# Two throw-away tiles for the squares, and a hand-built order with new constants

## The chip, the core and the metric

The kernel runs on one core of a Trainium2 chip. The core has five engines that run side by side, each through its own list of instructions in order: TensorE (PE, matrix products), VectorE (DVE), ScalarE (ACT, pointwise functions, copies and sums along a row), GpSimd (POOL) and SyncE (SP, which issues DMA transfers). They wait for each other by semaphores. TensorE's array can be used in parts; here two halves work on different things at once. The metric is the device time of one execution in microseconds (us), the median of several.

## What is computed

Four batches of 12608 tokens with 128 channels pass through an attention over 32 induced points in both directions, and every token then goes through a layer with 1024 hidden values:

```
def mab(q, kv):                                  # attention, softmax over the keys
    a = softmax(scale * q @ kv.T);  return a @ kv
h = mab(inducing, x)                             # 32 points look at all tokens of a batch
y = mab(x, h)                                    # each token looks at the 32 points
h1 = y @ w_in                                    # 128 -> 1024
solu = h1 * softmax(h1)
ln = (solu - mean(solu)) / sqrt(var(solu) + 1e-6) * g_ln
out = ln @ w_out                                 # 1024 -> 128
```

## The kernel before

Tokens are worked on in tiles of 128, 99 to a batch, 396 in all. Each tile goes round a ring of engines: PE forms the first layer (L974) into one of two PSUM buffers; DVE scales it, writes it to a row buffer and takes the row's extreme (L1009); ACT takes the exponential into a buffer `eu`, with its row sum (L1019); POOL multiplies the two (L1023); ACT squares the product for the variance and keeps only the row sum, so the squares themselves go to a throw-away tile `sq` (L1034); DVE transposes the product (L1047). Four tiles make a group; PE multiplies a transposed group by the output weights (L1093) in two streams, one on each half. The streams' results gather in two PSUM banks over three groups and are then evacuated to a tile of raw results by DVE or ACT (L1118), the variance is finished on ACT and POOL (L1145 to L1165), and the scaled output is written by ACT in four activations or by POOL in one operation (L1180, L1176) and stored. The function `p1` does the first attention of the next batch meanwhile, `p2` the second attention, twelve tiles at a time.

Nothing is scheduled on the chip. A `Planner`, when the program is built, keeps a clock for every engine, takes each step's cost from a number in the code, and writes out the instructions in the order in which its model would start them. Among steps that are ready within `SLACK` of the earliest it takes the one with the lowest priority number; the constants `PR_...` are offsets in tiles to that number, `P1_...`, `P2_...`, `LATE`, `WIN`, `WOUT` and `RUSH` place the work of the attentions and the weights, and `FILL` says from which gap on PE is kept busy with throw-away transposes. Where a step has an alternative (`alt`), the planner takes the engine that suits. `AFTER` is the delay from the end of a step on one engine to a start on another. The engines then run these lists in order. `HN_MORE` says how many of the spare buffers, left when the raw results have theirs, become row buffers.

Three lines carry the step that the change touches most:

```
sq = buf([P, FF], "sq", BF16)
...
"ACT", 1040, lambda: nc.scalar.activation(sq, e, AF.Square, scale=1.0 / 32.0, accum_out=G["qe"][:, s, 0:1]), d,
```

Of the kernel before, what the change touches and what calls it, by code (L numbers as in the profile page):

```python
# [10 lines left out]
BF16 = mybir.dt.bfloat16  # L11
U32 = mybir.dt.uint32
I32 = mybir.dt.int32
AF = mybir.ActivationFunctionType
# [5 lines left out]
P = 128  # L20
C = 128
M = 32
FF = 1024
# [5 lines left out]
JB = FF // M  # L29
BEAT = 224  # L30
SWITCH = 310


def cut(total, most, unit):
# [13 lines left out]
DIRECT = 3  # L48
EUS = 5
SPARES = 8  # L50
H_LAST = -34.17
TURNS = 3
ODD = 1
HN_MORE = 5
RAWS = 2
FILL = 358.31
FIRST = 4
LATE = -7.63
P1_FROM = 9.25
P1_GO = -11.78  # L60
P1_STEP = 6.49
P2_AHEAD = 40.84
P2_START = 24
PR_EX = 1.43
PR_EV = -19.77
PR_FI = 11.4
PR_G2 = -2.26
PR_HN = -3.18
PR_MU = -2.16
PR_SQ = 14.63  # L70
PR_SA = 24.36
PR_SP = 15.35
PR_ED = 14.54
PR_EA = -9.6
PR_TU = 2.38
RUSH = 2.52
TURN_NS = 62
PARTS = {"PE": ("PE0", "PE1")}
SLACK = {"PE": 17, "ACT": 71, "DVE": 138, "POOL": 33, "SP": 0}
SPARE = 150  # L80
WARM = 32
WOUT = -6.79
WIN = -19.36

AFTER = {
    "PE": {"PE": 0, "ACT": 237, "DVE": 236, "POOL": 240, "SP": 290},
# [16 lines left out]
class Done:  # L103


    def __init__(self, eng, end):
        self.eng, self.end = eng, end


class Op:  # L110
    def __init__(self, eng, cost, fn, *after, prio=None, alt=None, moves=0):
        self.eng, self.cost, self.fn, self.after, self.prio, self.alt, self.moves = eng, cost, fn, after, prio, alt, moves


class Event:
# [19 lines left out]
class Planner:  # L135
# [97 lines left out]
    def run(self):  # L233
        clock = self.clock
        while self.ops:
            first = min(self.ops, key=lambda o: (max(self.free(o[0].eng), o[1]), o[3]))
            eng = first[0].eng
            limit = max(self.free(eng), first[1]) + self.slack[kind(eng)]
            same = {eng, "PE"} if eng in PARTS["PE"] else {eng, *PARTS.get(eng, ())}
            pick = min(  # L240
                (o for o in self.ops if o[0].eng in same and o[1] <= limit),
                key=lambda o: (o[2][1] if o[0].prio is None else o[0].prio, o[3]),
            )
            self.ops = [o for o in self.ops if o[3] != pick[3]]
            op, ready, task = pick[:3]
            eng = op.eng
            start = max(self.free(eng), ready)
            if kind(eng) == "PE" and start - self.free("PE") > FILL:
                self._fill(start - SPARE)
            self.now = start  # L250
            op.fn()
            end = start + (self._pe(start, op.cost) if kind(eng) == "PE" else op.cost)
            for e in PARTS.get(eng, (eng,)):
                clock[e] = end
            if eng == "SP":
                end = self.data = max(end + DMA_LAG, self.data) + op.moves / DMA_RATE
            done = Done(eng, end)
            self._step(task, done)
        assert not self.blocked, "the plan is stuck"
# [3 lines left out]
def set_attention_then_solu_kernel(ctx: ExitStack, tc: tile.TileContext, x, inducing, w_in, w_out, g_ln, out):  # L263
    nc = tc.nc
    NB, N, _ = x.shape
    scale = 1.0 / float(C) ** 0.5
# [29 lines left out]
    def buf(shape, name, dtype=F32, where=None):  # L296
        return (where or const).tile(shape, dtype, name=name)

    def bufs(n, shape, name, dtype=F32):
        return [buf(shape, f"{name}{i}", dtype) for i in range(n)]  # L300
# [17 lines left out]
    where = bank_pool.__enter__()  # L318
    bank_e = [buf([P, 512], f"bank_e{i}", where=where) for i in range(8)]
    hn_b = bufs(3, [P, FF], "hn")  # L320
    sq = buf([P, FF], "sq", BF16)

    eu_b = buf([P, EUS, FF], "eu")
    xT_b = buf([C, PG, P], "xT")
# [143 lines left out]
    def weights_out():  # L468
# [11 lines left out]
        for k in range(KC):  # L480
            d = yield Op("ACT", 251, gain(k), g, gd, prio=LATE)
        g = [d]
        mp, rel = yield H

        def mean():
            for k in range(KC):
                nc.tensor.matmul(mp[:, :C], lhsT=ones_mean, rhs=wg[:, k, :], start=(k == 0), stop=(k == KC - 1))

        d = yield Op("PE", KC * 215, mean, g, rel, prio=LATE)
        d = yield Op(  # L490
# [3 lines left out]
            ),  # L494
            d, prio=LATE,
        )
# [7 lines left out]
        for a in range(4):  # L504
            for q in range(4):
                c = yield dma(
                    M * FF * 4,
                    lambda: nc.sync.dma_start(rows[a * M : (a + 1) * M, :, q, :C], wg[q * M : (q + 1) * M]), d, o, issue=600, prio=LATE,
                )
# [69 lines left out]
    def p1(b, k):  # L579
# [87 lines left out]

        d = yield Op("PE", (0 if early else SWITCH) + n * (72 if early else 60), scores, ready, rel, ind_ready.after)

# [18 lines left out]
        )  # L688
        d = yield Op("PE", (280 if early else SWITCH) + 110, lambda: nc.tensor.matmul(mq, lhsT=fold2, rhs=v["mdiag"], start=True, stop=True), d)
        first = k == 0  # L690
# [157 lines left out]
    def p2(b, j):  # L848
# [26 lines left out]

        d = yield Op("PE", 72 * n if direct else SWITCH + n * 60, scores, d, rel, hd)
        if not direct:
# [72 lines left out]
    def PRIO_P1(b, k):  # L950
        return -20.0 + k if b == 0 else NT * (b - 1) + P1_FROM + P1_STEP * k + P1_GO

# [3 lines left out]
    def main():  # L956
        for t, (b, j, s) in enumerate(tiles):
            for item in starts.get(t, ()):
                spawn(*item)
            G = grp[(b, j)]  # L960
            if s == 0:
                spawn(open_group(b, j), t)
            ka, i = part_of[b, ff_groups[j][0] + s]
            aT_d = yield aT_ready[(b, ff_groups[j][0] + s)]
            hw_d = yield hw_ready[b]
            hp, rel = yield H.at(t + H_LAST)
            A = aT_of[(b, ka)]
            aT, hs = A["aT"][0], hT[b][1]

            def halves():  # L970
                for k in range(2):
                    rows = slice((i % 2 * 2 + k) * M, (i % 2 * 2 + k + 1) * M)
                    cols = slice(k * 512, (k + 1) * 512)
                    nc.tensor.matmul(hp[:, cols], lhsT=aT[rows, i // 2, :], rhs=hs[rows, cols], start=True, stop=True)  # L974

            d = yield Op(f"PE{i % 2}", 870, halves, aT_d, hw_d, rel, prio=t - 50)
            if t + 1 == len(tiles) or tiles[t + 1][0] != b:
                give(HW, hT[b], d)
            spawn(soft(t, hp, d), t)
# [19 lines left out]
    def soft(t, hp, d):  # L999
        b, j, s = tiles[t]  # L1000
        G = grp[(b, j)]
        ka, i = part_of[b, ff_groups[j][0] + s]
        A = aT_of[(b, ka)]
        hn, rel = yield HN
        nm, mrel = yield NM
        rn = A["aT"][1][:, i : i + 1]
        d = yield Op(
            "DVE", 1208,
            lambda: nc.vector.tensor_scalar(out=hn, in0=hp, scalar1=rn, scalar2=None, op0=ALU.mult, op1=ALU.min, accum_out=nm),  # L1009
            d, rel, mrel, prio=t + PR_HN,  # L1010
        )
        give(H, hp, d)
        A["left"] -= 1
        if not A["left"]:
            give(AT, A["aT"], d)
        srel = yield G["st"]
        e, rel = yield EU
        de = yield Op(
            "ACT", 1133, lambda: nc.scalar.activation(e, hn, AF.Exp, bias=nm, scale=-1.0, accum_out=G["qe"][:, s, 1:2]), d, rel, srel,  # L1019
            prio=t + PR_EX,  # L1020
        )
        give(NM, nm, de)
        d = yield Op("POOL", 2330, lambda: nc.gpsimd.tensor_tensor(out=e, in0=hn, in1=e, op=ALU.mult), de, prio=t + PR_MU)  # L1023
        give(HN, hn, d)
        left = []

        def over(d):
            left.append(d)
            if len(left) == 2:
                give(EU, e, *left)  # L1030

        def square():
            ds = yield Op(
                "ACT", 1040, lambda: nc.scalar.activation(sq, e, AF.Square, scale=1.0 / 32.0, accum_out=G["qe"][:, s, 0:1]), d,  # L1034
                prio=t + PR_SQ,
            )
            G["squared"].append(ds)
            over(ds)
            if len(G["squared"]) == ff_groups[j][1]:
                yield from floor(b, j)  # L1040

        spawn(square(), t)
        n = ff_groups[j][1]
        rel = yield G["vt"]
        dt = yield Op(
            "DVE", 1163,
            lambda: nc.vector.transpose(  # L1047
                out=G["vtb"][:, : n * FF].rearrange("p (j s t) -> p j s t", j=M, s=n)[:, :, s, :],
                in_=e.rearrange("p (a f) -> p a f", f=M),
            ),  # L1050
            d, rel, prio=t + PR_TU,
        )
        over(dt)
        G["turned"].append(dt)
        if len(G["turned"]) == n:
            for w in range(2):
                spawn(products(b, j, t, w), t)
# [158 lines left out]
    for b in range(NB):  # L1216
        if b:
            for k in range(NP):
                starts.setdefault(NT * (b - 1) + int(P1_FROM + P1_STEP * k), []).append((p1(b, k), PRIO_P1(b, k)))
        starts.setdefault(max(0, NT * (b - 1)), []).append((combine(b), PRIO_P1(b, NP - 1) if b else -28))  # L1220
# [3 lines left out]
    def handover():  # L1224
# [23 lines left out]
        for i in range(at, SPARES):  # L1248
            give(HN if i < at + HN_MORE else EU, spare[:, more + i * FF : more + (i + 1) * FF], *done)
        for v in vt_b:  # L1250
# [51 lines left out]
```

## Time and profile before

| | us |
|---|---|
| median of 3 runs (lowest, highest) | 1207.19 (1206.87, 1208.22) |
| the profiled execution | 1207.56 |
| its span, first to last instruction | 1205.7 |
| PE busy, matmul | 1162.4 (96%) |
| ACT busy | 1138.5 (94%) |
| DVE busy | 1104.9 (92%) |
| POOL busy | 1073.9 (89%) |

A line of busy time is the time in which at least one instruction of that engine ran. PE counts as busy when either half works. An activation that accumulates shows as two rows, the activation itself and the read of its accumulator; neighbouring rows may overlap. In the timeline a row has start, duration, engine, line, operation, output and inputs, shape and count, and in brackets the idle time ahead of it with what ended it.

### The profile page before, as it was taken

How to read it: one execution, taken by the hardware profiler on the slowest of the kernel's cores; microseconds unless marked ns; L12 is line 12 of the kernel's file. 1: busy time of each engine (PE TensorE's matmuls, PEld its weight loads, DVE VectorE, ACT ScalarE, POOL GpSimd, SP SyncE). 2: the span in 40 equal slices, each digit the busy share in tenths (PEclk: the TensorE clock that was granted, in tenths of full speed). 3: DMA queues.
4: the chain of work that ended last, by engine and by line, in shares of the span. 5: the costliest groups of instructions: out<-in, count | busy, mean ns of one | idle time of the engine just before them, and what ended most of it. 6: DMA issues, size and time to landing. Idle time of an engine off the chain costs nothing.

```text
span 1205.7 us, 69282 instructions
## 1 busy us (share of the span) xinstructions
PE 1162.4 (96%) x30901; PEld 1041.7 (86%) x30901; DVE 1104.9 (92%) x1727; ACT 1138.5 (94%) x2396; POOL 1073.9 (89%) x790
## 2 busy tenths in 40 slices
PE   9889999999999999999999999999999999999996
PEld 7558989898899898888898988988888988889896
DVE  6799999999999999999999999999999999999992
ACT  5588999999999999999999999999999999999994
POOL 2678998889999999989799999999889999999994
PEclk9879999999999999999999999999999999999999
DMA  9453334432223433242223334233211212221011
GB/s 352 176 134 89 87 91 127 127 92 72 74 74 86 133 116 93 80 130 88 73 75 91 94 94 136 78 117 116 83 47 50 80 39 57 56 57 38 21 31 44
DMA packets 134252, 111.49 MB, mean 92 GB/s; under 512 B 79009, under 2 KB 87105, under 8 KB 133825
## 3 DMA queue, kind: packets, MB, share of 16 engines
q1 hardware_dynamic: 133952, 107.06, 30.4%
q8 instruction: 242, 3.96, 1.4%
q14 instruction: 58, 0.47, 0.1%
HBM read 53.51 MB, written 51.39 MB: 87 GB/s over the span
## 4 chain that ended last, share of the span: by engine, by line
PE 22%; ACT 19%; DVE 9%; issue 6%; POOL 1%; DMA 1%; SPq 0%; ACTq 0%; POOLq 0%; DVEq 0%
PE op L1093 17%; ACT eu L1019 8%; ACT sq L1034 7%; DVE vt L1047 3%; PE h L974 2%; DVE hn L1009 2%; DVE spare L1009 2%; ACT os L1180 1%; POOL eu L1023 1%; PE h L546 1%; ACT spare L1118 1%; DVE spare L1118 1%; ACT aT L915 1%; DMA dd<-qe 0%; ACT xT L608 0%
## 5 line engine op out<-in xcount | busy, mean ns | idle before, releaser
L1093 PEld LDWEIGHTS op<-wc,vt 32*128 32x128 f32 x25600 | 939.7, 186 | 63.0 <-issue 32.6
L1093 PE MATMUL op<-wc,vt 32*128 32x129 f32 x25600 | 978.6, 274 | 15.8 <-ACT spare L1118 6.6
L1023 POOL TENSOR_TENSOR eu<-spare,eu 128x1024 f32<-128x1024 f32 x249 | 586.2, 2373 | 27.3 <-ACT eu L1019 27.3
L1047 DVE STREAM_TRANSPOSE vt<-eu 128x1024 f32<-128x1024 f32 x396 | 484.8, 1233 | 7.1 <-POOL eu L1023 6.9
L1034 ACT ACTIVATE sq<-eu 128x1024 bf16<-128x1024 f32 x396 | 415.7, 1050 | 16.0 <-POOL eu L1023 4.4
L974 PE MATMUL h<-hs,aT 32*128 32x512 f32 x1584 | 416.2, 617 | 8.4 <-DVE spare L1009 3.0
L1023 POOL TENSOR_TENSOR eu<-hn,eu 128x1024 f32<-128x1024 f32 x147 | 346.4, 2371 | 16.4 <-ACT eu L1019 15.8
L1009 DVE TENSOR_SCALAR_CACHE_REDUCE spare<-h,rn 128x1024 f32<-128x1024 f32 x249 | 311.6, 1257 | 18.8 <-PE h L974 11.2
L1019 ACT ACTIVATE eu<-spare,nm 128x1024 f32<-128x1024 f32 x249 | 283.4, 1139 | 5.8 <-DVE spare L1009 4.8
L1009 DVE TENSOR_SCALAR_CACHE_REDUCE hn<-h,rn 128x1024 f32<-128x1024 f32 x147 | 184.2, 1259 | 12.8 <-PE h L974 10.6
L1019 ACT ACTIVATE eu<-hn,nm 128x1024 f32<-128x1024 f32 x147 | 167.3, 1139 | 0.7 <-DVE hn L1009 0.6
L974 PEld LDWEIGHTS h<-hs,aT 32*128 32x128 f32 x1584 | 124.6, 189 | 33.7 <-issue 8.6
L1180 ACT ACTIVATE os<-spare,fin 128x128 f32<-128x128 f32 (+1 forms) x264 | 82.9, 389 | 1.2 <-POOL fin L1165 1.2
L1034 ACT ACTIVATION_READ_ACCUMULATOR sq<-eu 128x1 f32 x396 | 74.6, 188 | 0.0
L1019 ACT ACTIVATION_READ_ACCUMULATOR eu<-spare,nm 128x1 f32 x249 | 47.0, 189 | 0.0
L546 PE MATMUL h<-ident,xn 32*128 32x32 f32 x1188 | 46.1, 219 | 0.8 <-issue 0.6
L546 PEld LDWEIGHTS h<-ident,xn 32*128 32x128 f32 x1188 | 45.2, 137 | 0.8 <-ACT xT L608 0.3
L1118 DVE COPY spare<-op 128x774 f32<-128x774 f32 (+1 forms) x31 | 27.5, 888 | 19.2 <-PE op L1093 12.0
L546 PEld LDWEIGHTS h<-ident,a 32*128 32x128 f32 (+1 forms) x800 | 34.5, 138 | 10.3 <-issue 3.2
L887 POOL TENSOR_TENSOR s<-s,mx 128x384 f32<-128x384 f32 (+3 forms) x37 | 28.7, 775 | 14.4 <-DVE mx L884 14.3
L608 ACT COPY xT<-h 128x768 f32<-128x768 f32 (+2 forms) x54 | 39.4, 729 | 1.1 <-PE h L546 1.0
L546 PE MATMUL h<-ident,a 32*128 32x32 f32 (+1 forms) x800 | 37.1, 219 | 3.2 <-DVE hn L1009 1.7
(160 smaller groups left out, 762.1 us busy)
## 6 DMA issues: line engine op xcount, KB each, us to landing
out_dram<-os SPq DMA_DIRECT2D x96, 256.0 KB, 2.5
xT<-xd SPq DMA_DIRECT2D x93, 256.0 KB, 3.2
xn<-in_x_dram SPq DMA_DIRECT2D x73, 256.0 KB, 3.0
xd<-xT SPq DMA_DIRECT2D x73, 256.0 KB, 2.6
dl<-dd SPq DMA_DIRECT2D x396, 1.0 KB, 2.7
xd<-vt SPq DMA_DIRECT2D x6, 768.0 KB, 10.4
spare<-in_x_dram SPq DMA_DIRECT2D x5, 768.0 KB, 10.7
wc<-hn SPq DMA_DIRECT2D x16, 128.0 KB, 3.0
```

Of the source, the lines that this page charges most:

```text
L546: nc.tensor.transpose(out=tr[:h, at : at + M], in_=block[rows, :h], identity=ident[rows, rows])
L608: nc.scalar.copy(in_rows(xT[:, :n, :], c0), from_rows(tr, n))
L887: lambda: nc.gpsimd.tensor_tensor(out=s2[:, :n, :], in0=s2[:, :n, :], in1=mx[:, :n].unsqueeze(2).to_broadcast([P, n, M]), op=ALU.subtract),
L974: nc.tensor.matmul(hp[:, cols], lhsT=aT[rows, i // 2, :], rhs=hs[rows, cols], start=True, stop=True)
L1009: lambda: nc.vector.tensor_scalar(out=hn, in0=hp, scalar1=rn, scalar2=None, op0=ALU.mult, op1=ALU.min, accum_out=nm),
L1019: "ACT", 1133, lambda: nc.scalar.activation(e, hn, AF.Exp, bias=nm, scale=-1.0, accum_out=G["qe"][:, s, 1:2]), d, rel, srel,
L1023: d = yield Op("POOL", 2330, lambda: nc.gpsimd.tensor_tensor(out=e, in0=hn, in1=e, op=ALU.mult), de, prio=t + PR_MU)
L1034: "ACT", 1040, lambda: nc.scalar.activation(sq, e, AF.Square, scale=1.0 / 32.0, accum_out=G["qe"][:, s, 0:1]), d,
L1047: lambda: nc.vector.transpose(out=G["vtb"][:, : n * FF].rearrange("p (j s t) -> p j s t", j=M, s=n)[:, :, s, :], in_=e.rearrange("p (a f) ...
L1093: nc.tensor.matmul(op[:rows, a - 2 * w, i * (C + 1) : (i + 1) * (C + 1)], lhsT=vt[q, k, :], rhs=wc[q, k, :], start=(k == 0), stop=(k == JB ...
L1118: return lambda: eng(F["raw"][:rows, : 4 * k, :].rearrange("p (j a) c -> p j a c", a=4)[:, :, 2 * w : 2 * w + 2].rearrange("p j a c -> p a ...
L1180: nc.scalar.activation(os[:rows, q, :], raw[:, q, :], AF.Copy, scale=y[:, i0 + q : i0 + q + 1])
```

## The change

The squares write two tiles in turn instead of one; a step can have a `tail`, a time by which the planner takes its result as ready later, and the first layer gets one of 80 ns; and most of the planner's constants have new values.

```
-H_LAST = -34.17
+H_LAST = -36.3
-HN_MORE = 5
+HN_MORE = 7
-FILL = 358.31
+FILL = 419.69
-LATE = -7.63
-P1_FROM = 9.25
-P1_GO = -11.78
+LATE = -20.28
+P1_FROM = 8.96
+P1_GO = -8.64
-PR_G2 = -2.26
...
-PR_SQ = 14.63
-PR_SA = 24.36
-PR_SP = 15.35
...
+PR_G2 = 4.93
...
+PR_SQ = 12.45
+PR_SA = 21.51
+PR_SP = 7.52
...
-RUSH = 2.52
+RUSH = 9.95
...
-SLACK = {"PE": 17, "ACT": 71, "DVE": 138, "POOL": 33, "SP": 0}
+SLACK = {"PE": 60, "ACT": 59, "DVE": 137, "POOL": 0, "SP": 0}
...
+            end += op.tail
             done = Done(eng, end)
...
-    sq = buf([P, FF], "sq", BF16)
+    sq_b = bufs(2, [P, FF], "sq", BF16)
...
-            d = yield Op(f"PE{i % 2}", 870, halves, aT_d, hw_d, rel, prio=t - 50)
+            d = yield Op(f"PE{i % 2}", 870, halves, aT_d, hw_d, rel, prio=t - 50, tail=TAIL)
...
+            def into():
+                sq_b.reverse()
+                nc.scalar.activation(sq_b[0], e, AF.Square, scale=1.0 / 32.0, accum_out=G["qe"][:, s, 0:1])
+
+            ds = yield Op("ACT", 1040, into, d, prio=t + PR_SQ)
```

The numbers of lines grow by 2 or 3 in the new file (L1034 is L1037, L1118 is L1121). The order of the instructions changes on every engine. Two places show how.

ACT near the end of the program, before: `sq` is the throw-away tile, `eu` a buffer of products, `fin` the small tiles of the variance, `x2` two equal rows on end.

```order
L1034 ACTIVATE sq,qe_104<-eu 128x1024
L1034 ACTIVATE sq,qe_106<-eu 128x1024
L1019 ACTIVATE eu,qe_108<-spare,nm_115 128x1024
L1019 ACTIVATE eu,qe_108<-spare,nm_116 128x1024
L1180 ACTIVATE os_101<-spare,fin_113 128x128 x4
L1034 ACTIVATE sq,qe_106<-eu 128x1024 x2
L1019 ACTIVATE eu,qe_108<-spare,nm_117 128x1024
L1034 ACTIVATE sq,qe_106<-eu 128x1024
L1034 ACTIVATE sq,qe_108<-eu 128x1024 x3
```

Five of these squares stand directly behind another one and write what it wrote. ACT in the same stretch now, with `sq_83` and `sq_84` the two tiles:

```order
L1037 ACTIVATE sq_84,qe_105<-eu 128x1024
L1037 ACTIVATE sq_83,qe_107<-eu 128x1024
L1021 ACTIVATE eu,qe_109<-spare,nm_116 128x1024
L1183 ACTIVATE os_102<-spare,fin_114 128x128 x4
L1021 ACTIVATE eu,qe_109<-spare,nm_117 128x1024
L1037 ACTIVATE sq_84,qe_107<-eu 128x1024
L1037 ACTIVATE sq_83,qe_107<-eu 128x1024
L1021 ACTIVATE eu,qe_109<-spare,nm_118 128x1024
L1037 ACTIVATE sq_84,qe_107<-eu 128x1024
L1037 ACTIVATE sq_83,qe_109<-eu 128x1024
L1037 ACTIVATE sq_84,qe_109<-eu 128x1024
L1037 ACTIVATE sq_83,qe_109<-eu 128x1024
```

Neighbouring squares no longer write the same tile. In the whole program a square stands directly behind a square 146 times before and 117 times now; of these, 146 and 30 wait on ACT's own semaphore.

ACT at the first evacuation, in the first batch, before (`op` is a bank of products, `spare` here the raw results):

```order
L1034 ACTIVATE sq,qe_102<-eu 128x1024
L1118 COPY spare<-op_667 128x2x3x129
L1118 COPY spare<-op_668 128x2x3x129
L1145 ACTIVATE fin_111<-dl_110,tiny 128x12
L1146 ACTIVATE fin_111<-spare 128x12
```

Both banks are evacuated by ACT, one behind the other. ACT at the same place now:

```order
L1037 ACTIVATE sq_83,qe_103<-eu 128x1024
L1121 COPY spare<-op_673 128x2x3x129
L1148 ACTIVATE fin_112<-dl_111,tiny 128x12
L1021 ACTIVATE eu,qe_105<-hn_82,nm_115 128x1024
L1149 ACTIVATE fin_112<-spare 128x12
```

ACT has one of the two. DVE has the other, between a transpose of `p1` (`ew`) and one of the ring (`vt`), and stands so:

```order
L1050 STREAM_TRANSPOSE vt<-eu 128x32x32
L1011 TENSOR_SCALAR hn_82,nm_115<-h_671,rn_96 128x1024
L737 STREAM_TRANSPOSE ew<-eT 128x384
L1121 COPY spare<-op_672 128x2x3x129
L1050 STREAM_TRANSPOSE vt<-eu 128x32x32
```

The second evacuation has moved to DVE. Over the program ACT has 41 evacuations before and 33 now, DVE 31 and 39; ACT 264 and 256 output scalings, POOL 34 and 36; DVE 21 and 24 of the running sums of `p1`, POOL 15 and 12. All other counts are the same, but for a few throw-away transposes on PE.

## Rows read from the trace of the kernel before

**Rows 1.** Busy time of each engine by stage; (x) is the number of instructions.

```profile
core 0: us, PE busy (x) PEld busy (x) DVE busy (x) ACT busy (x) POOL busy (x), PEclk, DMA share, GB/s
50.60:343.20 292.60, 286.39 (x7357) 248.19 (x7358) 271.67 (x429) 278.14 (x574) 261.88 (x179) 0.95 0.35 98
343.20:628.60 285.40, 281.93 (x7778) 255.02 (x7776) 273.02 (x426) 280.55 (x589) 263.79 (x195) 1.00 0.34 96
628.60:914.80 286.20, 281.88 (x7778) 256.16 (x7774) 272.53 (x426) 281.12 (x593) 264.82 (x194) 0.99 0.33 95
914.80:1180.00 265.20, 251.95 (x7012) 235.06 (x7008) 248.82 (x330) 260.35 (x548) 254.92 (x181) 0.98 0.17 45
1180.00:1206.00 26.00, 15.24 (x509) 14.66 (x501) 4.13 (x5) 10.12 (x28) 8.59 (x18) 0.91 0.14 40
```

**Rows 2.** Waits of ACT, 343.2 to 628.6 us: us in total, times, longest us.

```profile
ACT eu L1019 <- DVE spare L1009: 0.6, 1, 0.6
```

**Rows 3.** Waits of DVE, 343.2 to 628.6 us, the same columns.

```profile
DVE spare L1009 <- PE h L974: 3.6, 10, 0.9
DVE hn L1009 <- PE h L974: 1.8, 4, 0.9
```

**Rows 4.** Timeline of ACT, two stretches between 699 and 716 us.

```profile
699.28 1.05 ACT L1034 ACTIVATE sq<-eu 128x1024 bf16<-128x1024 f32 x1
700.23 0.20 ACT L1034 ACTIVATION_READ_ACCUMULATOR sq<-eu 128x1 f32 x1
700.52 1.06 ACT L1034 ACTIVATE sq<-eu 128x1024 bf16<-128x1024 f32 x1
...
701.58 1.13 ACT L1019 ACTIVATE eu<-spare,nm 128x1024 f32<-128x1024 f32 x1
...
712.50 1.14 ACT L1019 ACTIVATE eu<-spare,nm 128x1024 f32<-128x1024 f32 x1
713.53 0.19 ACT L1019 ACTIVATION_READ_ACCUMULATOR eu<-spare,nm 128x1 f32 x1
713.63 1.14 ACT L1019 ACTIVATE eu<-hn,nm 128x1024 f32<-128x1024 f32 x1
...
714.76 1.04 ACT L1034 ACTIVATE sq<-eu 128x1024 bf16<-128x1024 f32 x1
```

**Rows 5.** Groups by line and shape: count, busy us, mean ns, idle before.

```profile
L1176 POOL TENSOR_TENSOR os<-spare,fin 128x512 f32<-128x512 f32 x33 | 34.5, 1047 | 0.1
...
L1118 ACT COPY spare<-op 128x774 f32<-128x774 f32 x37 | 29.6, 799 | 4.5 <-DVE spare L1118 2.9 <-PE op L1093 0.7
...
L1118 DVE COPY spare<-op 128x774 f32<-128x774 f32 x27 | 25.8, 957 | 10.8 <-ACT spare L1118 6.9 <-PE op L1093 3.6
...
L724 DVE TENSOR_SCALAR l<-l,small 128x1 f32<-128x1 f32 x17 | 4.5, 267 | 1.5 <-ACT eT L715 1.1 <-ACT os L715 0.3
```

**Rows 6.** Timeline of ACT, four output scalings and the row behind them.

```profile
724.70 1.26 ACT L1180 ACTIVATE os<-spare,fin 128x128 f32<-128x128 f32 x4
725.87 0.20 ACT L900 ACTIVATE nr<-nr 128x12 f32<-128x12 f32 x1
```

**Rows 7.** Timeline of POOL at the end, its last four products.

```profile
1174.27 9.36 POOL L1023 TENSOR_TENSOR eu<-spare,eu 128x1024 f32<-128x1024 f32 x4
```

**Rows 8.** Waits of DVE, 50.6 to 343.2 us, the same columns.

```profile
DVE spare L1009 <- PE h L974: 5.1, 6, 1.7
DVE hn L1009 <- PE h L974: 3.3, 6, 1.3
```

**Rows 9.** Waits of POOL, 914.8 to 1180 us, the same columns.

```profile
POOL fin L1149 <- ACT fin L1146: 2.8, 3, 1.9
POOL s L887 <- DVE mx L884: 1.8, 1, 1.8
```

**Rows 10.** Timeline of PE near the end: a first-layer tile, a group.

```profile
1167.87 1.02 PE L974 MATMUL h<-hs,aT 32*128 32x512 f32 x4
...
1170.07 7.43 PE L1093 MATMUL op<-wc,vt 32*128 32x129 f32 x256
```

More of the change, by code (lines that the diff above doesn't have):

```diff
@@ L31 @@
 SWITCH = 310
+TAIL = 80
 def cut(total, most, unit):
@@ L63 @@
 P2_START = 24
-PR_EX = 1.43
+PR_EX = 1.59
 PR_EV = -19.77
-PR_FI = 11.4
-PR_G2 = -2.26
-PR_HN = -3.18
-PR_MU = -2.16
-PR_SQ = 14.63
-PR_SA = 24.36
-PR_SP = 15.35
-PR_ED = 14.54
-PR_EA = -9.6
-PR_TU = 2.38
-RUSH = 2.52
+PR_FI = 13.82
+PR_G2 = 4.93
+PR_HN = -3.97
+PR_MU = -3.64
+PR_SQ = 12.45
+PR_SA = 21.51
+PR_SP = 7.52
+PR_ED = 14.85
+PR_EA = -6.45
+PR_TU = 1.75
+RUSH = 9.95
 TURN_NS = 62
 PARTS = {"PE": ("PE0", "PE1")}
-SLACK = {"PE": 17, "ACT": 71, "DVE": 138, "POOL": 33, "SP": 0}
+SLACK = {"PE": 60, "ACT": 59, "DVE": 137, "POOL": 0, "SP": 0}
 SPARE = 150
 WARM = 32
-WOUT = -6.79
-WIN = -19.36
+WOUT = -7.05
+WIN = -18.04
 AFTER = {
@@ L110, with __init__ @@
 class Op:
-    def __init__(self, eng, cost, fn, *after, prio=None, alt=None, moves=0):
-        self.eng, self.cost, self.fn, self.after, self.prio, self.alt, self.moves = eng, cost, fn, after, prio, alt, moves
+    def __init__(self, eng, cost, fn, *after, prio=None, alt=None, moves=0, tail=0):
+        self.eng, self.cost, self.fn, self.after, self.prio, self.alt, self.moves, self.tail = eng, cost, fn, after, prio, alt, moves, tail
 class Event:
@@ L1032, in square @@
         def square():
[L1033 to L1036, printed above, removed]
+            def into():
+                sq_b.reverse()
+                nc.scalar.activation(sq_b[0], e, AF.Square, scale=1.0 / 32.0, accum_out=G["qe"][:, s, 0:1])
+            ds = yield Op("ACT", 1040, into, d, prio=t + PR_SQ)
             G["squared"].append(ds)
```

## The prediction

> **What bounds the kernel now.** Read first the busy time by stage, one stage for each of the four batches [rows 1]. A stage runs from the first exponential of its batch to that of the next, the last one to 1180 us. Call them B0 (292.6 us), B1 (285.4), B2 (286.2), B3 (265.2); before them lie 50.6 us of start, behind them 26 us of end. Subtract busy from length, and the idle time stands there. ACT: 14.5, 4.9, 5.1, 4.9 us. DVE: 20.9, 12.4, 13.7, 16.4. POOL: 30.7, 21.6, 21.4, 10.3. PE: 6.2, 3.5, 4.3, 13.3. So in B1 to B3 ACT is at 98%, and DVE and POOL have more room, POOL in B3 excepted (96%). PE counts as busy when one half of its array works, so its 98% alone is not yet a bound. The DMA engines are busy a third of the time, and SyncE issues the same 908 transfers before and after.
>
> Second view: what ACT waits for in B1 [rows 2]. The longest entry is 0.6 us in 285. Nobody holds ACT up; it simply has that much to do. DVE in the same stage waits 3.6 + 1.8 us for first-layer results from PE [rows 3]. That makes ACT the one to relieve, and DVE the next in line.
>
> Third view: ACT's own rows, one by one [rows 4]. An exponential starts at 712.50, the next at 713.63, a square at 714.76: 1.13 us apart, though each takes 1.14 and the read of its accumulator ends another 0.09 later, so neighbours overlap by 0.09 to 0.10 us. A square at 700.52 is followed by an exponential at 701.58, 1.06 us later. But the squares of 699.28 and 700.52 stand 1.24 us apart: the second starts 0.09 us after the read of the first has ended, with no overlap. Both write the one throw-away tile, and in the program of before each square directly behind a square, 146 of 396, waits on ACT's own semaphore. The exponentials, which write different tiles and accumulate too, show none of it. So **a square behind a square costs 0.18 us more** (1.24 - 1.06).
>
> **The change part by part.** *Two tiles in turn.* 146 x 0.18 = 26.3 us of ACT go: 38 such pairs in B0 (6.8 us), 33 in B1 (5.9), 34 in B2 (6.1), 41 in B3 (7.4). In the new order 117 pairs are left, 30 of which still carry a wait, for the square two back. That one has ended a whole square (1.05 us) earlier, so I take 0; the other end is 30 x 0.18 = 5.4 us given back.
>
> The Trainium skill, "ScalarE: Activation LUTs", section "What ACT_TABLE_LOAD costs", gives 93 ns as the overlap of back-to-back activations. The overlapping rows agree; by that figure alone a pair would give back 0.093, an estimate of 13.6 us in all. The rows show more, because the idle 0.09 goes too, and they decide.
>
> *Work that moves between engines.* I counted both orders. Evacuations of the product banks: ACT 41 to 33, DVE 31 to 39 (in B0 4, B1 2, B2 2, B3 0 move). One takes 0.80 us on ACT, of which 0.10 would overlap, so 0.70, and 0.96 on DVE [rows 5]. Output scalings (four activations for a group): 264 to 256 on ACT, 34 to 36 groups on POOL; by stage ACT has 20 fewer, 8 more, 8 more, 4 fewer. Four of them take 1.17 us from start to start [rows 6], 0.29 each, and a group costs POOL 1.05 [rows 5]. Three more running sums fall to DVE instead of POOL, at 0.27 each [rows 5]. The sums:
> ACT, relieved: B0 6.8 + 2.8 + 5.8 = 15.4; B1 5.9 + 1.4 - 2.3 = 5.0; B2 6.1 + 1.4 - 2.3 = 5.2; B3 7.4 + 1.2 = 8.6; together **34.2 us**.
> DVE, loaded: 8 x 0.96 + 3 x 0.27 = 8.5 us, of which B0 3.8, B1 some 2.2, B2 some 3.
> POOL: +5.3 in B0, -2.1 in B1, -2.1 and some sums less in B2, +1.1 in B3.
>
> *First-layer results later, constants anew.* The 80 ns change no instruction; they move DVE's reads of first-layer results behind other DVE work. DVE's waits for PE, 5.4 us in B1, can shrink by that; bounds 0 and 5.4 a stage, and I take 0 and let it serve as cover for the load on DVE. One constant has no effect: of the eight spare buffers three go to the raw results, five are left, and both 5 and 7 mean "all of them". The start is reordered (a block of twelve tiles of the second attention stands ahead of the first normalisation on DVE now), and the end is the same chain: POOL's last product ends at 1183.6 [rows 7], and behind it transpose, products, evacuation, scaling and store follow one by one, 22 us to the end of the span. Both at 0, within 2 us either way.
>
> *How much of the 34 arrives.* A stage shortens until the next engine is full.
> B1: ACT gives 5.0. DVE has 12.4 - 2.2 = 10.2 idle left, of which 5.4 are waits for PE that a faster ACT doesn't shorten: 4.8 to use. Both allow almost 5; but three engines near 98% at once, on few buffers, get into each other's way, so I take 3. B2 likewise 3.
> B0: ACT gives 15.4. DVE has 20.9 - 3.8 = 17.1 idle, 5.1 + 3.3 of it waits for PE [rows 8]: 8.7 to use, and I take 6.
> B3: ACT gives 8.6, but POOL has only 10.3 idle, 1.1 of it newly used, and of that some 4.6 us are waits for results of ACT and DVE [rows 9]. I take 3.
> Sum 6 + 3 + 3 + 3 = 15 us. The profiled execution took 1207.56 us (span 1205.7 and 1.9 around it): 1192.6. The median of the runs shown is 0.4 lower: **1192.2 us**, -1.2%.
>
> **The rivals.** *All of it comes through.* Each stage gives what ACT gives up, B0 until DVE's idle is down to a few us (about 11), B3 until POOL's waits are gone (5): 11 + 5 + 5 + 5 = 26, 1181. For it: ACT waits for nobody [rows 2], and relieving the bound moves the whole ring of DVE, ACT and POOL. Against it: four engines would all have to stand near 98%.
>
> *PE is the next bound.* 25 groups of products at 7.43 us with both halves at work, and 99 first-layer tiles at 1.02 us of one half [rows 10], are 186 + 50 = 236 us for each half in B1, ahead of transposes, scores and the first attention of the next batch, and PE idles 3.5 us there [rows 1]. If its halves are really that full, B1 and B2 give 1 each, B0 5, B3 2: 9 us, 1198.
>
> *The wait was not the tile's.* The stall might lie in something else that two squares share. Then pairs keep their 0.18, and only 29 fewer pairs (5.2 us) and the moved work (34.2 - 26.3 = 7.9) remain: 13 of 34 us, by the share above 6 us, 1201. Against it: neighbouring exponentials also accumulate into the same small tile, and overlap [rows 4].
> The Trainium skill, "VectorE: DVE Perf Modes", section "The DRAIN you can't avoid", measured chained operations with and without a semaphore between them and found that it costs nothing extra; were ACT like that, this rival would hold. The page speaks of VectorE, and the rows on ACT speak otherwise.
>
> *Slower: DVE becomes the bound and keeps its waits.* DVE's idle of the four stages, 63.4 us [rows 1], would have to be unavoidable: waits for PE, for POOL and for the evacuation on the other engine. Then its 8.5 us of added work lengthen the run: 1216. It decides where DVE's idle of B1 doesn't fall below 12 us. Against it: ACT is what delays the exponentials, and behind them DVE's transposes.
>
> **How the numbers follow.** Forecast 0.57 (1185 to 1199 by itself: what I took of each stage may be off by half), all through 0.13, PE 0.12, not the tile 0.08, DVE 0.10. Two per mille, 2.4 us, is about what a measurement of this kernel can tell from no change. The forecast and the full gain are faster; of the PE and the not-the-tile cases, 0.20 together and uncertain by 5 us, 0.14 are faster and 0.06 the same; of the DVE case 0.01 is the same and 0.09 slower. Faster 0.84, same 0.07, slower 0.09. The range from 1179 to 1207 takes in all but the slower case and a little at the low end.
>
> **What would show it.** In the profile after: squares behind squares 1.04 to 1.06 us apart (1.22 or more would refute the tile's step); ACT's total of busy and short idle down by 20 us or more; DVE 8 us busier, and its idle of B1 under 10 us; POOL waiting less for exponentials; stage lengths of some 287, 282, 283 and 262 us. Wrong it would be by a PE without idle and DVE waiting longer for first-layer results, or by evacuations that wait for each other on ACT: they share a tile of raw results, and DVE's now stands ahead.

## The result: 21 us faster, and the profile after

The changed kernel takes 1186.49 us (median of 4 runs, 1185.18 to 1186.94) against 1207.7 of before: a ratio of 0.982, interval 0.9803 to 0.9837. The forecast was 1192.2, the range 1179 to 1207. The direction held, and two tiles alone give about half of the gain (e1 below); the gain is 21 us where 15 was expected.

By stage, as in [rows 1], with one correction. The last stage is better cut where POOL's last product ends: in some orders POOL stands further behind at the last exponential, and a cut there would call that "end". Each line: stretch, length, busy time of every engine.

```profile
core 0: us, PE busy (x) PEld busy (x) DVE busy (x) ACT busy (x) POOL busy (x), PEclk, DMA share, GB/s
51.80:334.23 282.43, 277.52 (x7285) 244.33 (x7288) 269.23 (x423) 267.90 (x547) 264.07 (x183) 0.96 0.36 98
334.23:616.67 282.44, 280.91 (x7794) 253.42 (x7790) 275.20 (x431) 278.19 (x597) 264.57 (x193) 1.00 0.34 98
616.67:900.28 283.61, 281.98 (x7777) 256.70 (x7776) 273.45 (x428) 278.61 (x599) 261.18 (x187) 0.99 0.32 94
900.28:1163.30 263.02, 258.72 (x7212) 240.06 (x7208) 252.79 (x339) 258.26 (x551) 258.88 (x185) 1.00 0.19 48
```

For before, the same cut of the last stage is 914.82 to 1183.63, 268.8 us, and the end 22.0. So start, B0, B1, B2, last, end were 50.6, 292.5, 285.5, 286.2, 268.8, 22.0 and are 51.8, 282.4, 282.4, 283.6, 263.0, 21.6. The gains: -1.2, **10.1**, 3.0, 2.6, **5.8**, 0.4, together 20.8 of the span.

The squares that stood 1.24 us apart in [rows 4], in the timeline of after:

```profile
684.99 1.05 ACT L1037 ACTIVATE sq<-eu 128x1024 bf16<-128x1024 f32 x1
685.94 0.19 ACT L1037 ACTIVATION_READ_ACCUMULATOR sq<-eu 128x1 f32 x1
686.03 1.04 ACT L1037 ACTIVATE sq<-eu 128x1024 bf16<-128x1024 f32 x1
```

1.04 us from the first square to the second, and the read of the first (ending at 686.13) overlaps the second by 0.10. Of 117 such pairs in ACT's timeline 111 are between 1.04 and 1.06 us apart; the other six wait for POOL. In before the median was 1.23, in two groups: 33 of the 146 pairs stand 1.16 to 1.17 us apart and 113 stand 1.22 or more. In the 113 the second square also waits for POOL, and the trace has a separate wait instruction of ACT between the two squares; the 33 have none.

ACT's busy time fell from 1138.5 to 1117.8 us, DVE's rose from 1104.9 to 1109.1. The idle time of DVE in B1, 12.4 in [rows 1], is 282.44 - 275.20 = 7.2 now. In the last stage POOL is busy 258.9 of 263.0 us.

### The profile page after: what moved, and what is told of

It is laid out like the page before. It is cut to its first block, busy times and chain, and to the rows that moved or that the text cites. A ratio compares the mean times of both kernels' runs of the same rounds, so it can differ in the third digit from the quotient of the medians.

```text
span 1184.9 us, 69207 instructions
## 1 busy us (share of the span) xinstructions
PE 1156.9 (98%) x30908; PEld 1039.2 (88%) x30908; DVE 1109.1 (94%) x1738; ACT 1117.8 (94%) x2380; POOL 1074.5 (91%) x789
## 4 chain that ended last, share of the span: by engine, by line
PE 68%; DVE 14%; ACT 11%; issue 5%; DMA 1%; POOL 1%; POOLq 0%; ACTq 0%; DVEq 0%; SPq 0%
PE op L1096 51%; PE h L976 7%; DVE vt L1050 6%; ACT eu L1021 4%; ACT sq L1037 4%; DVE spare L1011 3%; PE h L548 3%; PE h L873 2%; PE h L748 2%; DVE hn L1011 2%; PE h L666 1%; DVE spare L1121 1%; DMA eu<-in_moe_w_out_dram 1%; ACT spare L1121 1%; ACT os L1183 1%
## 5 line engine op out<-in xcount | busy, mean ns | idle before, releaser
L1096 PEld LDWEIGHTS op<-wc,vt 32*128 32x128 f32 (+1 forms) x25600 | 932.9, 185 | 55.6 <-issue 30.9
L1096 PE MATMUL op<-wc,vt 32*128 32x129 f32 (+1 forms) x25600 | 972.2, 274 | 5.8 <-ACT spare L1121 2.8
L1025 POOL TENSOR_TENSOR eu<-spare,eu 128x1024 f32<-128x1024 f32 x249 | 587.1, 2373 | 22.6 <-ACT eu L1021 21.5
L1037 ACT ACTIVATE sq<-eu 128x1024 bf16<-128x1024 f32 x396 | 413.8, 1047 | 5.0 <-POOL eu L1025 4.5
L1025 POOL TENSOR_TENSOR eu<-hn,eu 128x1024 f32<-128x1024 f32 x147 | 347.7, 2374 | 20.5 <-ACT eu L1021 19.7
L976 PEld LDWEIGHTS h<-hs,aT 32*128 32x128 f32 x1584 | 122.9, 187 | 26.7 <-DVE spare L1011 10.3
L1183 ACT ACTIVATE os<-spare,fin 128x128 f32<-128x128 f32 (+1 forms) x256 | 80.4, 388 | 1.2 <-POOL fin L1168 1.2
L1037 ACT ACTIVATION_READ_ACCUMULATOR sq<-eu 128x1 f32 x396 | 75.5, 191 | 0.0
L1121 DVE COPY spare<-op 128x774 f32<-128x774 f32 (+1 forms) x39 | 35.2, 901 | 19.6 <-PE op L1096 12.2
L917 ACT COPY aT<-h 128x384 f32<-128x384 f32 (+3 forms) x82 | 32.4, 405 | 7.0 <-PE h L548 4.6
## 6 DMA issues: line engine op xcount, KB each, us to landing
xd<-vt SPq DMA_DIRECT2D x6, 768.0 KB, 10.3
spare<-in_x_dram SPq DMA_DIRECT2D x5, 768.0 KB, 10.5
```

The lines of the kernel that those rows point to most:

```text
L917: lambda: nc.scalar.copy(in_rows(aT[:h, qa:qb, :], w), from_rows(tr, nq)[:h, qa:qb]),
L1037: nc.scalar.activation(sq_b[0], e, AF.Square, scale=1.0 / 32.0, accum_out=G["qe"][:, s, 0:1])
L1096: nc.tensor.matmul(op[:rows, a - 2 * w, i * (C + 1) : (i + 1) * (C + 1)], lhsT=vt[q, k, :], rhs=wc[q, k, :], start=(k == 0), stop=(k == JB ...
L1121: return lambda: eng(F["raw"][:rows, : 4 * k, :].rearrange("p (j a) c -> p j a c", a=4)[:, :, 2 * w : 2 * w + 2].rearrange("p j a c -> p a ...
L1183: nc.scalar.activation(os[:rows, q, :], raw[:, q, :], AF.Copy, scale=y[:, i0 + q : i0 + q + 1])
```

## The experiments

Of before, the medians beside the runs were 1207.7 to 1208.8 us. The stage lengths of all kernels, read from each timeline as above (first exponential of each batch on ACT, end of POOL's last product, end of the span), in us:

| kernel | median | start | B0 | B1 | B2 | last | end |
|---|---|---|---|---|---|---|---|
| before | 1207.7 | 50.6 | 292.5 | 285.5 | 286.2 | 268.8 | 22.0 |
| e1 two tiles alone | 1197.27 | 50.6 | 291.9 | 281.7 | 282.3 | 264.7 | 22.1 |
| after | 1186.49 | 51.8 | 282.4 | 282.4 | 283.6 | 263.0 | 21.6 |
| e2 after, one tile | 1201.21 | 52.2 | 285.5 | 287.1 | 284.9 | 266.3 | 23.1 |
| e3 after, delay 0 | 1195.61 | 51.6 | 288.3 | 279.9 | 283.1 | 268.9 | 22.1 |
| e11 after, delay 100 | 1197.12 | 53.3 | 286.2 | 282.4 | 285.3 | 266.0 | 21.6 |
| e12 after, square at 1046 | 1196.05 | 53.3 | 282.1 | 284.6 | 288.5 | 265.7 | 21.5 |
| e4 before's constants, tiles, delay | 1209.52 | 51.2 | 293.6 | 288.0 | 287.9 | 268.0 | 21.7 |
| e5 after, less PE | 1180.68 | 52.3 | 283.2 | 282.5 | 278.7 | 263.0 | 21.1 |
| e6 after, less ACT | 1187.11 | 53.2 | 282.7 | 281.2 | 282.4 | 263.5 | 21.2 |
| e7 after, less DVE | 1186.63 | 53.2 | 282.8 | 282.1 | 281.3 | 263.4 | 21.3 |
| e8 after, less POOL | 1185.69 | 52.2 | 282.4 | 283.3 | 282.8 | 262.2 | 22.8 |
| e10 after, less of these three | 1179.57 | 52.2 | 283.3 | 281.5 | 282.4 | 258.3 | 21.9 |
| e9 before, less PE | 1207.73 | 50.3 | 293.2 | 287.0 | 286.5 | 268.0 | 21.1 |

Stage lengths are of one execution each; after and e6 to e8 share every list but for the cuts, and among them the start differs by up to 1.4 us and B2 by 2.3, so differences of that size can't be read. Of e5 to e8 and e10 there are two runs each.

**The tile alone (e1).** Every engine keeps its list of before.

```
-    sq = buf([P, FF], "sq", BF16)
+    sq_b = bufs(2, [P, FF], "sq", BF16)
```

(and the squares write `sq_b` in turn, as in the change)

> The kernel before with two throw-away tiles for the squares and nothing else; every engine keeps its list of instructions. If the wait on the one tile is what holds a square behind a square, the 146 pairs go from 1.23 to 1.04 us from start to start, 26 us of ACT. If ACT bounds the order of before, half or more of that arrives: 1190 to 1197 us. If the gain lies in the new order and the constants, this one stays at 1204 to 1208 us. If the stall is not the tile's, the pairs stay at 1.22 us or more and the time at 1207.

1197.27 us, ratio 0.9905 (0.989 to 0.992): half of the whole gain, with no instruction moved, and 0.3 us above the expected range. Of the 146 pairs 139 now stand 1.04 to 1.05 us apart. The stages:

```profile
50.61:342.50 291.89, 285.76 (x7345) 249.30 (x7349) 271.71 (x429) 274.81 (x574) 261.35 (x179) 0.95 0.36 99
342.50:624.20 281.70, 279.22 (x7767) 253.50 (x7765) 272.30 (x426) 277.52 (x591) 263.48 (x194) 1.00 0.34 98
624.20:906.49 282.29, 280.59 (x7776) 254.88 (x7774) 272.50 (x426) 278.59 (x593) 264.70 (x194) 0.99 0.34 96
906.49:1171.19 264.70, 254.29 (x7163) 237.25 (x7162) 250.53 (x331) 260.44 (x554) 259.14 (x183) 0.99 0.17 45
```

B1, B2 and the last stage give 3.8, 3.9 and 4.1 us; B0 gives 0.6, though 38 of the pairs lie in it. ACT's busy time in B0 falls from 278.14 to 274.81, but its idle rises from 14.5 to 17.1: the relief is not used.

**One tile in the new order (e2).** The reverse.

```
-    sq_b = bufs(2, [P, FF], "sq", BF16)
+    sq_b = bufs(1, [P, FF], "sq", BF16)
```

> The changed kernel with one throw-away tile; lists unchanged. 117 squares stand directly behind a square, so 117 x 0.18 = 21 us of ACT come back. If the tile carries the gain: 1196 to 1204 us. If the new order carries it: below 1190 us.

1201.21 us, 14.7 more than after, for 117 pairs at 0.18 = 21 us of ACT. The stall is back, in the timeline of ACT:

```profile
693.77 1.04 ACT L1037 ACTIVATE sq<-eu 128x1024 bf16<-128x1024 f32 x1
694.72 0.19 ACT L1037 ACTIVATION_READ_ACCUMULATOR sq<-eu 128x1 f32 x1
694.94 1.06 ACT L1037 ACTIVATE sq<-eu 128x1024 bf16<-128x1024 f32 x1
```

1.17 us here, 1.23 in the median of the 117. By e1 the tile is worth 0.4 of the ACT time that it frees, by e2 0.7, and the rival "the wait was not the tile's" is out. It follows too that the new order with one tile still beats before by 7 us (0.9936, 0.9918 to 0.9954).

**Without the delay of 80 ns (e3), and with 100 (e11).**

```
-TAIL = 80
+TAIL = 0
```

(100 in e11)

> The changed kernel with first-layer results taken as ready without the 80 ns; the new constants stay, so the order differs on all engines. If the 80 ns matter, DVE waits for first-layer results grow from 9 us between 90 and 1158 us to some 20 again and the time to 1192 or more. If only the tile and ACT's load matter: 1183 to 1190 us.

> The changed kernel with first-layer results taken as ready 100 ns later instead of 80; the order changes on all engines. If the delay helps by keeping DVE from waiting, 100 is as good as 80 within 3 us: 1184 to 1190. If the constants are a fit to one order and any other order costs what 0 ns did: 1192 to 1200.

1195.61 and 1197.12 us: both 9 to 11 us worse than 80. If the delay had worked by keeping DVE from waiting for first-layer results, 100 would have done nearly as well as 80. Without the delay those waits were expected to grow from 9 us to some 20, between 90 and 1158 us. They hardly grew: DVE in e3,

```profile
DVE spare L1011 <- PE h L976: 7.7, 15, 1.2
DVE hn L1011 <- PE h L976: 2.8, 5, 0.9
```

10.5 us against 9.1 (4.3 + 4.8) in after, and in e11 5.6 us (3.5 + 2.1). So these waits are not what makes the two 9 to 11 us slower. The order on every engine, SyncE's transfers included, differs in both. The loss of e3 lies in B0 and in the last stage (B1 is 2.5 us shorter), that of e11 in B0, the last stage and less in B2; its B1 is as long as that of after.

**A cost in the planner brought nearer to the chip (e12).**

```
-            ds = yield Op("ACT", 1040, into, d, prio=t + PR_SQ)
+            ds = yield Op("ACT", 1046, into, d, prio=t + PR_SQ)
```

> The changed kernel with the planner's cost of a square at 1046 ns instead of 1040; a square took 1047 in the profile, so that the number is nearer to the chip, and it changes no instruction, only the order. If the gain of order and constants comes from a closer model: 1184 to 1188 us. If it is a fit to one order: 1192 or more.

1196.05 us, 9.6 worse, with the same work but for some alternatives taken otherwise. Most of it is lost in B2 and the last stage. Two lines of the busy time by stage, of e3 in B0 and of e12 in B2, against 282.43 and 283.61 of after:

```profile
51.60:339.90 288.30, 282.08 (x7287) 244.69 (x7289) 273.16 (x427) 270.72 (x557) 261.72 (x178) 0.96 0.36 96
```

```profile
619.94:908.43 288.49, 284.60 (x7770) 254.63 (x7772) 274.26 (x431) 276.38 (x584) 266.87 (x194) 0.99 0.33 95
```

Against after, ACT's share of the stage falls from 94.9% to 93.9% in B0 and from 98.2% to 95.8% in B2, and DVE (94.7% and 95.1%), POOL (90.8% and 92.5%) and PE (97.8% and 98.7%, against 98.3% and 99.4% in after) don't fill the stage in its place. That the time lies between the engines and not on one of them is argued from these shares; PE counts as busy when one half is, so PE is not excluded by its share.

**The tile and the delay with the constants of before (e4).** The change without its constants.

```
+TAIL = 80
...
+            d = yield Op(f"PE{i % 2}", 870, halves, aT_d, hw_d, rel, prio=t - 50, tail=TAIL)
```

(and the two tiles)

> The constants of before with two tiles and the 80 ns: the change without the constants. If the constants were needed, it stands at 1195 us or more, near the tiles alone; if tile and 80 ns are all of it, at 1184 to 1190 us. DVE's waits for first-layer results should fall under 12 us if the 80 ns do what they say.

1209.52 us, no better than before, 12 worse than the tiles alone. And DVE's waits, expected under 12 us, grew: who waited for whom (us in total, times, longest us) in the whole of e4,

```profile
ACT eu L1021 <- DVE spare L1011: 16.1, 13, 3.0
...
DVE spare L1011 <- PE h L976: 15.2, 20, 1.9
```

ACT waits 16.1 us for DVE at the exponentials from spare buffers (4.8 in before, 5.7 in e1), and DVE 15.2 for first-layer results on their way there (11.2 and 11.9); with those for the row buffers `hn` it is 25.5 us (21.8 and 17.4). e4 differs from e1 by the delay alone, and in the order that follows from it.

**What bounds the kernel after (e5 to e8, e10) and before (e9).** Each takes work from an engine, 16 to 23 us as measured or worked out, and leaves the lists otherwise as they are.

```
+            if k < JB - 1:                                   # e5, and e9 on before: PE
+                nc.tensor.matmul(..., stop=(k == JB - 2))
...
+                nc.scalar.activation(sq_b[0][:, :960], e[:, :960], AF.Square, ...)      # e6: ACT
...
+                out=G["vtb"]...[:, :30, s, :],  in_=e...[:, :30, :],                    # e7: DVE
...
+        nc.gpsimd.tensor_tensor(out=e[:, :1000], in0=hn[:, :1000], in1=e[:, :1000], op=ALU.mult)   # e8: POOL
```

> The changed kernel, lists unchanged but for PE: the last of the 32 steps of every group's product is left out in both streams, 100 x 0.23 = 23 us of each half of PE (the output lacks that part). If PE bounds the changed kernel, 8 us or more of it arrive: below 1179 us. If PE has room, under 3 us: 1183 to 1187.

> The changed kernel with squares over 960 of 1024 columns, 396 x 0.053 = 21 us less of ACT (the variance lacks these columns). If ACT still bounds it: 1172 to 1179 us. If the bound has passed to DVE, POOL or PE: 1182 to 1187.

> The changed kernel with transposes of 960 of 1024 columns, some 396 x 0.07 = 28 us less of DVE (the products read old data there). If DVE is the bound now: below 1176 us. If not: 1182 to 1187.

> The changed kernel with POOL's product over 1000 of 1024 columns, 396 x 0.055 = 22 us less of POOL (the last columns keep the exponential). POOL is at 98% in the last batch only: 3 to 5 us there and next to nothing before, 1180 to 1184 us. If POOL bounds all batches: below 1175.

> The changed kernel with all three cuts at once: squares over 960 columns, transposes over 960, products of POOL over 1000 (output wrong in these parts); PE and all lists unchanged. If PE and its waits in the list bound it: 1181 to 1187 us. If ACT, DVE and POOL bound it together, so that one alone can't help: below 1175 us.

> The kernel before with the last of the 32 steps of every group's product left out in both streams, 23 us of each half of PE (the output lacks that part); the lists are otherwise those of before. If ACT alone bounds it, as the prediction had it: under 3 us, 1204 to 1208 us. If PE held it back as well: 6 us or more, below 1202, as much as the same cut gave the changed kernel (5.8).

The first line of the page's busy time, of e6, e7, e8 and e10 in this order, shows that the cuts were made (of after: DVE 1109.1, ACT 1117.8, POOL 1074.5); for PE the count of matmuls does, 30108 in e5 and 30101 in e9, 800 fewer than in after and before:

```profile
PE 1154.6 (98%) x30908; PEld 1037.2 (88%) x30908; DVE 1108.3 (94%) x1738; ACT 1101.9 (93%) x2380; POOL 1075.0 (91%) x789
```

```profile
PE 1154.0 (97%) x30908; PEld 1036.0 (87%) x30908; DVE 1088.1 (92%) x1738; ACT 1116.5 (94%) x2380; POOL 1075.3 (91%) x789
```

```profile
PE 1157.1 (98%) x30908; PEld 1038.9 (88%) x30908; DVE 1108.7 (94%) x1738; ACT 1117.0 (94%) x2380; POOL 1055.3 (89%) x789
```

```profile
PE 1153.3 (98%) x30908; PEld 1037.9 (88%) x30908; DVE 1085.4 (92%) x1738; ACT 1100.5 (93%) x2380; POOL 1054.6 (89%) x789
```

Less ACT, less DVE, less POOL: 1187.11, 1186.63 and 1185.69 us, no difference from 1186.49. (Of POOL, busy 258.9 of 263.0 us in the last stage, 3 to 5 us had been expected there; the stage is 0.8 shorter.) All three together give 7 us, 4.7 of it in the last stage: 1179.57 falls between the two expectations. Less PE gives 5.8 of its 23 us, between the expectations too. In the profiled execution, 4.2 us shorter than that of after, B2 alone is 4.9 shorter, and ACT and PE both fill it:

```profile
617.87:896.60 278.73, 278.01 (x7570) 251.89 (x7567) 270.97 (x428) 277.73 (x599) 261.21 (x187) 1.00 0.33 96
```

ACT's idle time there is 1.0 us where after had 5.0. No run took work from PE and ACT together. The same cut of PE on the kernel before gives nothing (ratio 0.9991, 0.9973 to 1.001), while there 26 us of ACT gave 11.

So in the order of before ACT counted and PE did not, as read from [rows 2]. That ACT alone held it is not shown: B0 hardly gained by its relief (e1), and DVE and POOL were not relieved there. In the order of after no engine, relieved alone, gives a clear gain in more than one stage. ACT is near its limit there all the same: 21 us put back on it cost 14.7 (e2), 16 us taken off it gave nothing (e6). The chain that ended last does not tell that by itself; the page's shares, of before and of after:

```profile
PE 22%; ACT 19%; DVE 9%; issue 6%; POOL 1%; DMA 1%; SPq 0%; ACTq 0%; POOLq 0%; DVEq 0%
```

```profile
PE 68%; DVE 14%; ACT 11%; issue 5%; DMA 1%; POOL 1%; POOLq 0%; ACTq 0%; DVEq 0%; SPq 0%
```

The chain of before is followed back only to 499 us and its shares add up to 58% of the span, so PE has 22 of 58 there, 38%, against 68% in after. Even so, leaving out one step of 32 moved one stage of four. I expected e5 and e10 to name PE or the other three; neither does for all stages. What holds B0 and B1 in the order of after stays open.

## Why the prediction was right, and where it was off

*The stall (0.18 us for a square behind a square, gone with two tiles).* Right: 1.04 us in after and e1, 1.17 to 1.23 again in e2. The 33 pairs at 1.16 to 1.17 cost 0.12 instead of 0.18, so the 26.3 us of the sum were nearer to 25. The 30 pairs that still carry a wait cost nothing, as taken, or at least 24 of them: all but six of the 117 pairs stand 1.04 to 1.06 us apart.

*ACT as the bound, DVE next.* Supported for B1, B2 and the last stage of before by e1 and e9, not for B0. DVE as the next one was not shown: less DVE gave nothing (e7), and its added load did not decide, as its idle of B1 fell to 7.2 us, below the 12 at which the slower rival began. DVE's busy time rose by 4.2 us where 8.5 was worked out. The work did come: the durations of DVE's rows, added up one by one, grow by 8.9 us (1215.1 to 1224.0), 7.7 of it in full evacuations; neighbouring rows overlap more. PE's idle time in B1 and B2, 3.5 and 4.3 us, is 1.5 and 1.6 now. That is half of the sign that was named against the forecast; the other half, DVE waiting longer for first-layer results, did not come.

*How much arrives.* B1 and B2 were taken at 3 each and came to 3.0 and 2.6; the tile alone gives 3.8 and 3.9 there, and the rest of the change takes 0.7 and 1.3 back, differences within the spread of single executions. Two terms were too small. B0 was taken at 6 and gave 10.1, and less by the tile, which had 6.8 of the 15.4 us of ACT there (0.6 in e1, 3.1 from e2 to after), than by the new order: ACT's busy time falls by 10.2 us there, the length by 10.1, and ACT's idle (14.5 in both) stays. The sum had held B0 back by DVE's 8.4 us of waits for PE, which a faster ACT would not shorten. It did not (9.4 in e1), but the new order did: in after 3.9 are left (2.4 + 1.5). The last stage was taken at 3, since POOL's waits in [rows 9] seemed mostly beyond ACT's reach; cut at POOL's last product it gave 5.8, 4.1 of it by the tile. POOL's busy time there is the same in before (258.5) and after (258.9), but its idle time falls from 10.3 to 4.1 us, and of 6.2 us of waits up to the last exponential 0.4 are left (1.8 in e1). So they were within ACT's reach. The busy time of the stage in before, and all that POOL waits for in after up to the last exponential:

```profile
914.82:1183.63 268.81, 255.56 (x7142) 238.68 (x7139) 250.29 (x331) 263.78 (x553) 258.53 (x182) 0.98 0.17 44
```

```profile
POOL s L889 <- DVE mx L886: 0.4, 1, 0.4
```

POOL waiting less for exponentials, a sign that was named, came only in part: 41.2 us over the run against 43.1, with 11.3 for 20.5 in B0 and more than before in B1 and B2.

*The delay and the constants at 0.* This is the step that was off. With the tile alone at 1197.27 us, everything else is worth another 10.8 us. Most of it lies in B0: even with one tile the new order is 7.0 us shorter there than before (e2). What in the new order does it stays open. ACT's busy time in B0 (267.9 us in after, 269.8 in e11, 270.7 in e3, 271.6 in e4) and the stage's length (282.4, 286.2, 288.3, 293.6) rise together, but 3.7 us of load stand beside 11.2 of length, so the work moved off ACT is not all of it; no run moved it alone. DVE's waits for first-layer results, for which 0 was taken, fell from 21.8 to 10.3 us over the run; but e11 has 7.6 without the gain. The delay by itself it isn't: 0 and 100 ns, and an unrelated 6 ns in another cost, all land at 1195.6 to 1197.1, where the tile alone stands. That is what a set of constants fitted to one order would do. That the fit was made against measured times was not shown; the runs show only that its neighbours don't share the gain.

*The rivals.* "All of it" (1181) didn't come. "Not the tile's" is refuted by e1 and e2. "PE is the next bound" has support in B2 alone, from one execution (e5), and its 1198 did not come. "DVE keeps its waits" is refuted. Evacuations that wait for each other were named as a danger; in after ACT waits 0.9 us for DVE's evacuations between 90 and 1158 us, and DVE 6.8 for ACT's (6.9 in before, [rows 5]), so they cost no more than they did.

## What to carry to other kernels

A throw-away output is still an output: when ScalarE writes it twice in a row, the second write waits for the first, here 0.12 to 0.18 us each time. Look for start-to-start times of neighbours that miss the usual overlap, on the engine that waits for nobody, and give such outputs a second buffer. A static order that was fitted to a cost model should be measured again after every edit to the model, since edits of 6 or 20 ns moved this kernel by 10 us; and of an engine that fills a chain, cut a little work and measure before calling it the bound.

## What was not expected of the hardware

An engine at 98% of a stage may be no bound by itself. In B1 of the kernel after ACT is busy 278.2 of 282.4 us, and taking 16 us of busy time from it over the run left the time as it was (e6); the same held for 21 us of DVE and 19 us of POOL.
